# P times V in 64x32 tiles of TensorE, over two PSUM banks, with all eight banks in one pool

## The chip, the cores and the metric

The kernel runs on one core of a Trainium2 chip. Its time is the device time of one execution in microseconds (us). The kernel before takes 312.37 us (median of three runs, 312.09 to 313.11).

A core has a matrix engine, TensorE (PE in the profile, with its weight loads as PEld), three engines for elementwise work, VectorE (DVE), ScalarE (ACT) and GpSimd (POOL), and a queue that starts most transfers, SyncE (SP). TensorE adds up its results in PSUM, which has eight banks; one bank holds 512 float32 numbers in each of 128 partitions. VectorE and ScalarE read PSUM; the other working memory is SBUF.

## The reference

Two blocks read the same normalised input, and their outputs are added to the input. The sizes are S = 2048 rows, D = 640, F = 1536, 32 heads of 20 columns, and a window of 256 keys.

```python
xn = _layernorm(x, axis=-1)
return x + _A_ref(xn, A_wqkv, A_wo) + _B_ref(xn, B_w_gate, B_w_up, B_w_down)

# _A_ref: attention in a sliding window
qkv = (x @ wqkv).reshape(B, S, 3, H, Dh)            # q, k, v: 32 heads of 20
scores = jnp.einsum("bhqd,bhkd->bhqk", q, k) * (Dh ** -0.5)
mask = (idx[:, None] - idx[None, :] >= 0) & (idx[:, None] - idx[None, :] < W)   # W = 256
p = _softmax(jnp.where(mask, scores, -1e9), axis=-1)
return einsum("bhqk,bhkd->bhqd", p, v).transpose(...).reshape(B, S, D) @ wo

# _B_ref: gated feed-forward
h = _sigmoid(x @ w_gate) * (x @ w_up)
return h @ w_down
```

## The kernel before

The 2048 rows are worked in four chunks of 512 (c = 0 to 3). For each chunk there are projections to q and k (`proj_block`, L302), to v (`project_v`, L330), the gate and up products (`g_gu`, L412 and L419), the down product (`down`, L433), the product with `wo` (`add_wo`, L440), and the attention. Heads are taken in eight groups of four (g = 0 to 7).

Attention is cut into steps. `scores` (L478) computes one step: it writes scores with the keys on the partitions and the queries in columns, for four heads into four banks, one head to a bank. Queries are counted in blocks of U = 64. A piece (g, hf, r, q, n, col) stands for 64 keys (half hf of the key block r) against n query blocks from block q, put at column block col. Its four matmuls, one for each head, use tiles of TensorE of 32 rows by 64 columns: the head picks one of four row groups, hf one of two column groups. So eight tiles are in use, and two pieces of different hf can stream side by side. One ScalarE instruction (L490) then takes the exponential of all four banks, 2048 columns, into the SBUF tile pT; GpSimd (`keep`, L493) sets masked entries to zero. The chunk 0 has 16 "wide" steps, two to a group; the chunks 1 to 3 have two wide steps to a group, and one "full" step without masks for each pair of groups: 76 steps in all.

`pv` (L510) multiplies P by V for one group. A piece there takes all 128 keys of a block: its four matmuls (L519), one for each head, use tiles of 128 rows by 32 columns, four of them, side by side, and all add into one bank, `acc`. Because a piece has 128 keys in a row, both halves need the same query blocks. The oldest and newest query blocks of a wide step are wanted for one half only, so GpSimd copies them, masked, to two more column blocks of pT (the entry "late", the tile has 10 blocks of 64 where PSUM has 8), and `pv` runs pieces over these. For two groups of chunks 1 to 3 that makes 80 matmuls, for two groups of chunk 0 56. `finish_group` (L527) transposes `acc` on VectorE (L529) into SBUF; `scale_group` (L535) divides by the sum of each row (L537, L541) and transposes back into `oc` (L545), of which five tiles make up a chunk, and which `add_wo` multiplies with `wo`.

The program's order is written out by hand. The loop at L718 goes through the 76 steps; between two steps it pulls "fill" (the class Fill), pieces of the projections and of the feed-forward work, by a budget of TensorE time. Before some steps (the table `due`, L710) it runs `pv` for two groups, one step after the pair's last scores (two in chunk 0). There are 15 such places in the loop, and one at the end (L760). The scaling that follows is put in a list (`fill.behind`) and issued one or two at a time with the next pieces of fill. The output of a chunk is the fill `g_out` (L464): for each of four blocks of 128 rows it computes both halves of the down product in two banks, then adds both halves of the product with `wo`, adds x (`add_x`, L444) and stores the rows.

The PSUM banks are split between two pools. `ps_d` holds four, for everything but the scores, in turn; a pool of four, `ps_h`, serves transposes at the start, and is closed for `ps_s`, one buffer of four banks for the scores, which is closed for `ps_y` at the end.

Of the kernel before, what the change touches and what calls it, by code (L numbers as in the profile page):

```python
# [9 lines left out]
P = 128  # L10
# [34 lines left out]

SPAN = 5


def wide_step(g, r, old):  # L60

    q = 2 * r
    if old:
        return dict(scores=[(g, 0, r, q, 5, 1), (g, 1, r, q + 1, 5, 2), (g, 0, r + 2, q + 4, 2, 6),
                            (g, 1, r - 2, q, 2, 0), (g, 0, r - 2, q, 1, 0), (g, 1, r + 2, q + 5, 1, 7)],
                    late=(1, 8, 2), diag=1, oldest=(0, 2),
                    pv=[(g, r, q, 5, 1), (g, r + 2, q + 4, 2, 6), (g, r, q + 5, 1, 9),
                        (g, r - 2, q, 2, 0, 8)])

    scores = [(g, 0, r, q, 5, 0), (g, 1, r, q, 6, 0)]  # L70
    if r == 0:
        scores += [(g, 0, 2, 4, 3, 5), (g, 1, 2, 5, 2, 6)]
        last = [(g, 2, 4, 3, 5)]
    else:
        scores += [(g, 0, 3, 6, 2, 5), (g, 1, 3, 7, 1, 6), (g, 0, 2, 7, 1, 7), (g, 1, 2, 7, 1, 7)]
        last = [(g, 3, 6, 2, 5), (g, 2, 7, 1, 7)]
    return dict(scores=scores, late=(5, 9, 1), diag=0, oldest=(4, 1),
                pv=[(g, r, q, 5, 0), (g, r, q + 5, 1, 9)] + last)


def full_step(gs):

    pieces = [(g, r, q, 2, 4 * n + col) for n, g in enumerate(gs) for r, q, col in ((-1, 0, 0), (2, 6, 2))]
    return dict(scores=[(g, hf, *rest) for g, *rest in pieces for hf in range(2)], pv=pieces)
# [23 lines left out]
def kernel(  # L108
# [33 lines left out]
    ps_d = pool("ps_d", 4, space=bass.MemoryType.PSUM)  # L142
    banks = ctx.enter_context(ExitStack())
    ps_h = banks.enter_context(tc.tile_pool(name="ps_h", bufs=4, space=bass.MemoryType.PSUM))

    ctx.enter_context(tc.manual_schedule())


# [94 lines left out]
    for n in (6, 4):  # L243
        ps = ps_d.tile([P, CW], FP32, name="pwarm", tag="d")
        for k in range(n):
            nc.tensor.matmul(ps, lhsT=ones[:, 0:P], rhs=ones, start=(k == 0), stop=(k == n - 1))
# [32 lines left out]
    def transpose_rows(s, copy, lo=0, hi=DC):  # L279
        pt = ps_h.tile([P, DC, P], BF16, name="pt")  # L280
        for d in range(lo, hi):
            nc.tensor.transpose(pt[:, d, :], xns[0, s][:, d * P:(d + 1) * P], ident)  # L282
        copy(out=xnT[0][:, lo:hi, s * P:(s + 1) * P], in_=pt[:, lo:hi, :])

# [10 lines left out]
    def proj_block(w, c, m):  # L295
# [3 lines left out]
        ps = ps_d.tile([P, CW], FP32, name="pqk", tag="d")  # L299
        for d in range(DC):  # L300
            wt = wqkv[:, d, base:base + D].rearrange("p (k m) -> p m k", m=DC)
            nc.tensor.matmul(ps, lhsT=wt[:, m, :], rhs=xnT[c][:, d, :],  # L302
                             start=(d == 0), stop=(d == DC - 1))
        st = stp.tile([P, CW], BF16, name="st")
        if w == "q":
            nc.vector.tensor_copy(out=st, in_=ps)
        else:
            nc.scalar.copy(out=st, in_=ps)
# [17 lines left out]
    def project_v(c, s, hf, lo=0, hi=DC, ps=None):  # L326
        if ps is None:
            ps = ps_d.tile([P, CW], FP32, name="pv", tag="d")
        for d in range(lo, hi):
            nc.tensor.matmul(ps[:, 0:HALF], lhsT=xnT[c][:, d, s * P:(s + 1) * P],  # L330
                             rhs=wqkv[:, d, 2 * D + hf * HALF:2 * D + (hf + 1) * HALF],
                             start=(d == 0), stop=(d == DC - 1))
        return ps

    def copy_v(c, s, hf, ps, copy):
        v3 = vt[c * SBC + s][:, 0:H * VW].rearrange("p (h d) -> p h d", d=VW)
        copy(out=v3[:, hf * 16:(hf + 1) * 16, 0:DH],
             in_=ps[:, 0:HALF].rearrange("p (h d) -> p h d", d=DH))
# [69 lines left out]
    def g_gu(c, f0, f1):  # L408
        for f in range(f0, f1):
            pg = ps_d.tile([P, CW], FP32, name="pg", tag="d")  # L410
            for d in range(DC):
                nc.tensor.matmul(pg, lhsT=part(wg, d, f), rhs=xnT[c][:, d, :],  # L412
                                 start=(d == 0), stop=(d == DC - 1))
            th = tp.tile([P, CW], FP32, name="th")
            nc.scalar.activation(out=th, in_=pg, func=TANH, scale=0.5)  # L415
            yield 5 * MM
            pu = ps_d.tile([P, CW], FP32, name="pu", tag="d")
            for d in range(DC):
                nc.tensor.matmul(pu, lhsT=part(wu, d, f), rhs=xnT[c][:, d, :],  # L419
# [3 lines left out]
            nc.vector.scalar_tensor_tensor(out=h, in0=th, scalar=1.0, in1=pu, op0=ADD, op1=MULT)  # L423
# [7 lines left out]
    def down(c, s, y, cut):  # L431
        for f in range(FC):
            nc.tensor.matmul(y[:, 0:cut[1] - cut[0]], lhsT=ht[c, f][:, s * P:(s + 1) * P],  # L433
# [370 lines left out]
```

## Time and profile before

| | us |
|---|---|
| median of three runs | 312.37 (312.09 to 313.11) |
| profiled execution, span from the first to the last instruction | 310.6 |
| TensorE busy (matmuls) | 303.6 (98%) |
| ScalarE busy | 192.5 (62%) |
| VectorE busy | 159.0 (51%) |
| GpSimd busy | 155.4 (50%) |
| exponentials (L490), 76 | 142.7 busy, 1.878 each |
| masks (L493), 192 | 146.8 busy |
| transposes of `acc` (L529), 32 | 21.8 busy, 0.709 each |

The profiled execution's own time is its span, 310.6 us; the runs' median has 1.8 us more, which lies around the span. The profile gives a matmul a modelled end, so the busy share of TensorE counts some overlap twice; the pace is read from starts. In the timeline a row shows the start, the time from the first start to the last end of the rows merged in it, the engine and the line. In the chain of waits (the work that ended last, followed back) a row shows the start and the time that this work adds to the chain.

### The profile page before, as it was taken

Reading aid. Unit: us, or ns where it says so; the run is one execution under the profiler, and the core shown is the slowest. Engines: PE = TensorE matmul, PEld = TensorE weight load, DVE = VectorE, ACT = ScalarE, POOL = GpSimd, SP = SyncE. Lnnn points to the kernel's source line nnn. Section 1 sums busy time; section 2 is a strip of 40 time slices with the busy share of each in tenths; the row PEclk is TensorE's granted clock in tenths of the full one; section 3 lists DMA queues with packets and bytes.
Section 4 is the critical chain, followed back from the end, with each engine's and each line's share of the span. In section 5 each row is a group of like instructions: output and inputs, shape, how many; then the busy total and the mean of one; then the engine's idle time right before and its main releaser. Section 6 shows DMA issues by size and latency. Waiting matters only on the chain.

```text
span 310.6 us, 10139 instructions
## 1 busy us (share of the span) xinstructions
PE 303.6 (98%) x4436; PEld 175.0 (56%) x4471; DVE 159.0 (51%) x313; ACT 192.5 (62%) x179; POOL 155.4 (50%) x239
## 2 busy tenths in 40 slices
PE   7999999999999999999999999999999999999996
PEld 3654444556557655644567665644546675454775
DVE  5533655639775154289826155272733526272423
ACT  6623878697763747787673647767585547768000
POOL 3000675676782827567382637546273846656000
PEclk9999999999999999999999999999999999999999
DMA  7997999765534153440035212450000220000302
GB/s 219 367 298 253 321 182 318 258 185 170 177 65 108 44 160 100 164 151 2 2 44 87 88 59 88 154 190 2 2 3 2 66 64 23 2 2 2 88 22 65
DMA packets 40301, 35.69 MB, mean 115 GB/s; under 512 B 10400, under 2 KB 39712, under 8 KB 40224
## 3 DMA queue, kind: packets, MB, share of 16 engines
q1 hardware_dynamic: 39392, 34.27, 37.6%
q10 hardware_dynamic: 864, 0.77, 0.9%
q8 instruction: 35, 0.57, 0.8%
q14 instruction: 10, 0.08, 0.1%
HBM read 23.63 MB, written 10.26 MB: 109 GB/s over the span
## 4 chain that ended last, share of the span: by engine, by line
PE 96%; issue 1%; DMA 1%; ACT 1%; DVE 0%; SPq 0%
PE y L433 17%; PE pu L419 17%; PE pg L412 17%; PE pqk L302 14%; PE ps L485 9%; PE pv L330 7%; PE y L440 7%; PE acc L519 7%; DMA xc<-in_A_x_dram 1%; PE pt L282 0%; ACT xn L614 0%; ACT xn L619 0%; DVE xn L625 0%; SPq L171 0%; ACT rstd L620 0%
## 5 line engine op out<-in xcount | busy, mean ns | idle before, releaser
L493 POOL TENSOR_SCALAR_AFFINE_SELECT pT<-pT 128x512 bf16<-128x512 bf16 (+2 forms) x192 | 146.8, 795 | 128.3 <-ACT pT L490 128.1
L490 ACT ACTIVATE pT<-ps 128x2048 bf16<-128x2048 f32 x76 | 142.7, 1878 | 64.3 <-PE ps L485 59.4
L423 DVE SCALAR_TENSOR_TENSOR h<-th,pu 128x512 bf16<-128x512 f32 x48 | 32.7, 683 | 58.2 <-PE pu L419 43.6
L419 PE MATMUL pu<-xnT,wu 128*128 128x512 bf16 x228 | 59.2, 380 | 0.7
L412 PE MATMUL pg<-xnT,wg 128*128 128x512 bf16 x226 | 58.0, 380 | 0.9 <-issue 0.5
L433 PE MATMUL y<-wd,h 128*128 128x320 bf16 (+2 forms) x396 | 57.0, 295 | 0.0
L302 PE MATMUL pqk<-xnT,wqkv 128*128 128x512 bf16 x191 | 45.7, 381 | 0.7 <-issue 0.2
L433 PEld LDWEIGHTS <-h 128*128 128x128 bf16 x396 | 36.6, 98 | 14.4
L415 ACT ACTIVATE th<-pg 128x512 f32<-128x512 f32 x48 | 28.6, 596 | 14.4 <-PE pg L412 14.0
L412 PEld LDWEIGHTS <-wg 128*128 128x128 bf16 x240 | 22.2, 98 | 25.2 <-issue 0.2
L419 PEld LDWEIGHTS <-wu 128*128 128x128 bf16 x240 | 21.9, 98 | 25.4 <-issue 0.6
L485 PEld LDWEIGHTS <-kT 20*64 20x64 bf16 x1856 | 20.6, 103 | 24.2 <-issue 22.3
L302 PEld LDWEIGHTS <-wqkv 128*128 128x128 bf16 x200 | 22.5, 119 | 18.4 <-issue 1.0
L529 DVE STREAM_TRANSPOSE t<-acc 128x512 f32<-128x512 f32 x32 | 21.8, 709 | 21.5 <-PE acc L519 21.2
L444 DVE SCALAR_TENSOR_TENSOR rows<-y,rows 128x320 bf16<-128x320 f32 x30 | 14.5, 490 | 35.2 <-PE y L440 30.2
L485 PE MATMUL ps<-qT,kT 20*64 20x128 bf16 (+4 forms) x1856 | 32.5, 239 | 0.0
L541 DVE TENSOR_TENSOR on<-t,rec 128x320 bf16<-128x320 f32 (+4 forms) x48 | 27.1, 565 | 1.1
L440 PE MATMUL y<-wo,oc 128*128 128x320 bf16 (+2 forms) x165 | 24.2, 295 | 0.0
L330 PE MATMUL pv<-wqkv,xnT 128*128 128x320 bf16 x160 | 23.7, 299 | 0.0
L519 PE MATMUL acc<-pT,v 128*32 128x128 bf16 (+3 forms) x1184 | 22.9, 231 | 0.0
L519 PEld LDWEIGHTS <-v 128*32 128x32 bf16 x1184 | 18.5, 97 | 7.5 <-issue 2.2
L440 PEld LDWEIGHTS <-oc 128*128 128x128 bf16 x165 | 15.5, 98 | 5.9
(45 smaller groups left out, 132.2 us busy)
## 6 DMA issues: line engine op xcount, KB each, us to landing
qT<-sq SPq DMA_DIRECT2D x7, 512.0 KB, 4.3
sq<-st SPq DMA_DIRECT2D x20, 128.0 KB, 3.6
sk<-st SPq DMA_DIRECT2D x20, 128.0 KB, 4.1
out_dram<-rows SPq DMA_DIRECT2D x15, 160.0 KB, 1.8
kT<-sk SPq DMA_DIRECT2D x4, 512.0 KB, 7.4
wg<-in_B_w_gate_dram SPq DMA_DIRECT2D x4, 480.0 KB, 7.1
wu<-in_B_w_up_dram SPq DMA_DIRECT2D x4, 480.0 KB, 6.1
xc<-in_A_x_dram SPq DMA_DIRECT2D x3, 640.0 KB, 5.5
```

Source lines behind the costliest of these rows:

```text
L302: nc.tensor.matmul(ps, lhsT=wt[:, m, :], rhs=xnT[c][:, d, :], start=(d == 0), stop=(d == DC - 1))
L330: nc.tensor.matmul(ps[:, 0:HALF], lhsT=xnT[c][:, d, s * P:(s + 1) * P], rhs=wqkv[:, d, 2 * D + hf * HALF:2 * D + (hf + 1) * HALF], start=( ...
L412: nc.tensor.matmul(pg, lhsT=part(wg, d, f), rhs=xnT[c][:, d, :], start=(d == 0), stop=(d == DC - 1))
L415: nc.scalar.activation(out=th, in_=pg, func=TANH, scale=0.5)
L419: nc.tensor.matmul(pu, lhsT=part(wu, d, f), rhs=xnT[c][:, d, :], start=(d == 0), stop=(d == DC - 1))
L423: nc.vector.scalar_tensor_tensor(out=h, in0=th, scalar=1.0, in1=pu, op0=ADD, op1=MULT)
L433: nc.tensor.matmul(y[:, 0:cut[1] - cut[0]], lhsT=ht[c, f][:, s * P:(s + 1) * P], rhs=wd[:, f, cut[0]:cut[1]], start=(f == 0), stop=False)
L440: nc.tensor.matmul(y[:, 0:cut[1] - cut[0]], lhsT=oc[c, m][:, s * P:(s + 1) * P], rhs=wo[:, m, cut[0]:cut[1]], start=False, stop=(m == DC - 1))
L485: nc.tensor.matmul(ps[hf * U:(hf + 1) * U, i, col * U:(col + n) * U], lhsT=qk["k", kc, g // GH][32 * i:32 * i + DH, g % GH, key:key + U], ...
L490: nc.scalar.activation(out=pt[:, :, 0:CW], in_=ps, func=EXP, scale=SCALE)
L493: nc.gpsimd.affine_select(out=out, in_=in_, pattern=[[0, HG], [0, n], [sign, width]], compare_op=GE, fill=0.0, base=base, channel_multipli ...
L519: nc.tensor.matmul(acc[32 * i:32 * i + 32, q * U:(q + n) * U], lhsT=v[:, h * VW:h * VW + 32], rhs=cols[:, i, col:col + (n - 1) * by + 1:by ...
```

## The change

P times V is cut into halves of 64 keys, with the same pieces as the scores. `pv` uses tiles of 64 rows by 32 columns, eight of them: the half of the keys picks one of two row groups, the head one of four column groups. The two halves add into two PSUM banks. `finish_group` copies the one bank to SBUF on ScalarE, adds the other on VectorE, and transposes the sum from SBUF. The copies of column blocks by GpSimd are gone, and the masks are cut anew, some over 64 partitions. In chunks 1 to 3 a pair of groups has 128 matmuls in `pv`, in chunk 0 80.

The PSUM pools become one tile of eight banks, and a list `free` in which a released bank goes to the end. Scores take four of the first six (or first four, after `pv`) banks of the list, in one run if they can. Before `pv` the fill is run on until every bank has been given back (`fill.close`), and the four banks for `pv` are chosen among the first six. `g_out` finishes a half with `wo` before it begins the next half.

```diff
 def wide_step(g, r, old):
     q = 2 * r
     if old:
-        return dict(scores=[(g, 0, r, q, 5, 1), (g, 1, r, q + 1, 5, 2), (g, 0, r + 2, q + 4, 2, 6),
-                            (g, 1, r - 2, q, 2, 0), (g, 0, r - 2, q, 1, 0), (g, 1, r + 2, q + 5, 1, 7)],
-                    late=(1, 8, 2), diag=1, oldest=(0, 2),
-                    pv=[(g, r, q, 5, 1), (g, r + 2, q + 4, 2, 6), (g, r, q + 5, 1, 9),
-                        (g, r - 2, q, 2, 0, 8)])
+        scores = [(g, 0, r, q, 5, 1), (g, 1, r, q + 1, 5, 2), (g, 0, r + 2, q + 4, 2, 6),
+                  (g, 1, r - 2, q, 2, 0), (g, 0, r - 2, q, 1, 0), (g, 1, r + 2, q + 5, 1, 7)]
+        return dict(scores=scores, pv=scores, diag=1, cut=[], oldest=(0, 2))
...
+    ps = psp.tile([P, BANKS, CW], FP32, name="ps")
+    free = list(range(BANKS))
+
+    def new_banks(n, near):
+        got = min(itertools.combinations(sorted(free[:near]), n), key=runs)
+        for k in got:
+            free.remove(k)
+        return got
+
+    def acc_first(n, near):
+        got = min(itertools.combinations(free[:near], n),
+                  key=lambda ks: runs(sorted(set(free) - set(ks))))
+        free[:] = [*got, *(k for k in free if k not in got)]
...
-            ys = [ps_d.tile([P, CW], FP32, name=f"y{i}", tag="d") for i in range(2)]
-            for y, cut in zip(ys, HALVES):
+            for cut in HALVES:
+                y = new_bank()
                 yield from down(c, s, y, cut)
-            if s == 0:
-                yield from between
-            outp(c, s, ys, rows)
-            yield 10 * 136
+                if s == 0 and cut == HALVES[0]:
+                    yield from between
+                add_wo(c, s, y, cut)
+                add_x(y, cut, rows)
+                if cut == HALVES[1]:
+                    store(c, s, rows)
+                yield 5 * 136
...
-        if "late" in step:
-            src, to, n = step["late"]
-            keep(pt[:, :, to * U:(to + n) * U].rearrange("p h (n u) -> p h n u", u=U),
-                 spans(src, n, 1), n, U, -1 - U, -1)
-            u, n = step["oldest"]
-            keep(spans(u, n, 1), spans(u, n, 1), n, U, -1, -1)
-            keep(spans(step["diag"], 2, 2), spans(step["diag"], 2, 2), 2, P, 0, 1)
+        if "diag" in step:
+            u, (o, n) = step["diag"], step["oldest"]
+            keep(spans(u + 1, 2), U, 1)
+            keep(spans(o, n), -1, -1)
+            keep(spans(o + 1, n, U, P), -1, -1)
+            keep(spans(u, 2, 0, U), 0, 1)
+            for col in step["cut"]:
+                keep(spans(col, 1, U, P), -1 - P, -1)
         return pt

     def pv(c, g, parts):
-        acc = ps_d.tile([P, CW], FP32, name="acc", tag="d")
+        halves = [new_bank() for _ in range(2)]
...
-                    acc[32 * i:32 * i + 32, q * U:(q + n) * U],
-                    lhsT=v[:, h * VW:h * VW + 32], rhs=cols[:, i, col:col + (n - 1) * by + 1:by, :],
-                    start=(k == 0), stop=(k == len(flat) - 1), skip_group_check=True)
-        finish_group(c, g, acc)
+                    ps[32 * i:32 * i + 32, halves[hf], q * U:(q + n) * U],
+                    lhsT=v[hf * U:(hf + 1) * U, h * VW:h * VW + 32],
+                    rhs=pt[hf * U:(hf + 1) * U, i, col * U:(col + n) * U],
+                    start=(k == first[hf]), stop=(k == last[hf]), skip_group_check=True)
+        finish_group(c, g, halves)

-    def finish_group(c, g, acc):
+    def finish_group(c, g, halves):
+        t0 = lop.tile([P, CW], FP32, name="t0")
         t1 = np_.tile([P, 16, 32], FP32, name="t1")
-        nc.vector.transpose(out=t1.rearrange("p b r -> p (b r)"), in_=acc)
+        nc.scalar.copy(out=t0, in_=ps[:, halves[0], :])
+        nc.vector.tensor_tensor(out=t0, in0=ps[:, halves[1], :], in1=t0, op=ADD)
+        for k in halves:
+            give(k)
+        nc.vector.transpose(out=t1.rearrange("p b r -> p (b r)"), in_=t0)
...
+        def close(self):
+            while len(free) < BANKS:
+                self.one()
...
         if t in due:
+            fill.close()
             fill.flush()
+            acc_first(2 * len(due[t]), len(free) - 2)
...
-        made = (step, scores(c, step))
+        made = (step, scores(c, step, HG if t in due else 6))
```

## The prediction

> **What bounds the kernel now.** I read the busy shares first, then the chain of waits, then the waits, then stretches of the timeline around `pv`.
>
> Busy shares and the chain, by engine and by line:
>
> ```profile
> PE 303.6 (98%) x4436; PEld 175.0 (56%) x4471; DVE 159.0 (51%) x313; ACT 192.5 (62%) x179; POOL 155.4 (50%) x239
> ...
> PE 96%; issue 1%; DMA 1%; ACT 1%; DVE 0%; SPq 0%
> PE y L433 17%; PE pu L419 17%; PE pg L412 17%; PE pqk L302 14%; PE ps L485 9%; PE pv L330 7%; PE y L440 7%; PE acc L519 7%; DMA xc<-in_A_x_dram 1%; PE pt L282 0%; ACT xn L614 0%; ACT xn L619 0%; DVE xn L625 0%; SPq L171 0%; ACT rstd L620 0%
> ```
>
> The chain is TensorE for 96%, and no other engine is over 62% busy. So a microsecond less on TensorE is a microsecond less of time, if no wait takes its place; 7%, some 21.7 us, is `pv`.
>
> The waits of TensorE on others:
>
> ```profile
> PEld L485 <- issue: 22.3, 61, 0.4
> ...
> PEld L519 <- issue: 2.2, 7, 0.4
> ...
> PEld L519 <- ACT pT L490: 1.7, 4, 0.4
> ```
>
> All are 0.4 at longest: that is the change of tile shape, no wait for data. The timeline around a score step shows it:
>
> ```profile
> 151.19 1.24 PE L419 MATMUL pu<-xnT,wu 128*128 128x512 bf16 x5
> ...
> 152.36 0.43 PE L485 MATMUL ps<-qT,kT 20*64 20x320 bf16 x24
> 152.72 1.25 PE L412 MATMUL pg<-xnT,wg 128*128 128x512 bf16 x5
> 152.97 1.88 ACT L490 ACTIVATE pT<-ps 128x2048 bf16<-128x2048 f32 x1 [0.98 <-PE ps L485]
> ```
>
> Five matmuls of 512 columns take 1.08 (the chain's row below, 0.216 each). So they end at 152.27, and the scores start 0.09 later: the change of shape. Scores start to next start is 0.36: 0.09 for changing back and 0.27 of streaming. Each tile then streams 5 + 2 + 1 blocks of 64 = 512 columns, which at full pace take 0.216. So eight tiles do run side by side here, with 0.05 lost in a step. Scores end at 152.63; the exponential starts 0.34 later.
>
> The chain's rows for `pv` in chunk 0, and in a later chunk with a product and a score step:
>
> ```profile
> 81.72 1.11 PE acc L519 x56
> ```
> ```profile
> 151.35 1.08 PE pu L419 x5
> 152.43 0.36 PE ps L485 x24
> ...
> 164.85 1.45 PE acc L519 x80
> ```
>
> Each holds one change of shape, so streaming is 1.02 and 1.36. A pair of groups later than chunk 0 has 48 blocks in each tile = 3072 columns = 6 x 0.216 = 1.30, plus 0.06. Chunk 0 has 36 blocks = 2304 columns = 0.97, plus 0.05.
>
> **The change, part by part.** The counts of other matmuls, score steps and changes of shape (169) stay, so do the DMAs and their order on SP; 0 for these.
>
> *Streaming of `pv`.* With halves apart and both row groups busy, a later pair needs 4 wide steps of 8 blocks and 8 blocks of the full step: 40 blocks = 2560 columns = 1.08. Chunk 0 needs 32 blocks = 2048 columns = 0.86. To this comes the loss: 0.05 per pair as now, at most 0.05 for every three rounds as in a score step (16 rounds, 0.29). I take 0.08, nearest to the `pv` row, whose 20 rounds are the like of these. That gives 1.16 against 1.36 and 0.94 against 1.02: 12 x 0.20 + 4 x 0.08 = 2.7 us gained; 3.2 with 0.05, and nothing with a third of 0.05 for each round (1.37 and 1.03).
>
> [...]
>
> *The first refill of a bank.* ScalarE must now copy one half (32 copies of 128x512; the nearest row, tanh L415, is 0.596), and VectorE add the other (nearest L423, 0.683). The bank of the first half is the first that the fill takes after the scores that follow `pv`. From that half's end TensorE has the second group (0.58) and a score step with both changes (0.45) to do: 1.03, in chunk 0 0.92. Needed are 0.2 to 0.34 until ScalarE starts (tanh and scores rows), 0.6 for the copy and 0.05 to restart: 0.85 to 0.99. So it is covered by 0.04 to 0.18, and about even in chunk 0, if ScalarE is free. Its rows around the 16 calls show it free by then, save in the third, where casts of k end 0.95 after `pv` starts. I take 0.2 us for all 16; bounds 0 and 16 x 0.15 = 2.4. The second half's bank is wanted a fill piece (1.08) later, the add ends 0.7 after the copy: covered.
>
> *ScalarE's queue.* The next exponential stands behind the two copies. The second ends 0.8 after `pv` (0.2 + 0.6), where the scores, which end 0.36 after it, would let the exponential start 0.63 to 0.70 after it: 0.1 to 0.2 later against the scores. Behind it stand tanh and the next exponential, on which the next score step waits for its banks. In the stretch above it ends at 154.85 and the next scores start at 154.98, so the margin is 0.13; four `pv` calls now also take banks of the step before. I take 0.1 in all; 0 to 0.8.
>
> *VectorE and `oc` in the first output.* After `pv` VectorE has add, transpose, add, transpose, then both scalings. The cover is fill, save in the output of chunk 0, where `g_out` now wants `oc` after one half, not two. VectorE and ScalarE there, before:
>
> ```profile
> 82.06 0.69 DVE L423 SCALAR_TENSOR_TENSOR h<-th,pu 128x512 bf16<-128x512 f32 x1 [0.89 <-ACT th L415]
> 82.66 1.30 DVE L529 STREAM_TRANSPOSE t<-acc 128x512 f32<-128x512 f32 x2
> 83.89 0.21 DVE L537 RECIPROCAL rec<-t 128x16 f32<-128x16 f32 x1
> ...
> 85.34 0.24 DVE L537 RECIPROCAL rec<-t 128x16 f32<-128x16 f32 x1
> ...
> 86.37 0.71 DVE L545 STREAM_TRANSPOSE oc<-on 128x512 bf16<-128x512 bf16 x1
> ```
> ```profile
> 81.43 0.59 ACT L415 ACTIVATE th<-pg 128x512 f32<-128x512 f32 x1
> ```
>
> With `pv` at 81.65: the first copy runs 82.32 to 82.92, four VectorE instructions at 0.65 (this row's pace) from 82.98 to 85.6, the scalings take 1.45 and 1.74 as here: the last `oc` is there at 88.8 (87.08 now). TensorE reaches the fifth `wo` matmul, which reads it, after 0.94 (`pv`) + 0.45 (scores) + 12 x 0.136 (down) + 1.08 + 0.45 + 1.08 + 0.54 = 6.17, at 87.8. So it waits 1.0 us; nothing is behind it that others want soon. Bounds: 0 if one VectorE instruction less stands in front and the rest runs closer, 1.7 with one more. At the outputs of chunks 1 and 2 more than 10 us of fill lie between. At the end the last `oc` is there at 296.4, 4.0 after `pv`, and wanted 7.3 after it, behind 48 down matmuls; a copy (0.8) and two adds (1.3) more make 6.1: 0.
>
> *Masks.* GpSimd has four instructions of 512 (0.687) where a later wide step had 687 + 687 + 1103 ns: 2.75 against 2.48 us, some of them on 64 partitions. A full step and its fill lie between the last masks and `pv`, over 5 us: 0. Chunk 0's masks go from 2.1 to at most 2.9 us in steps of 2.6, with two steps before `pv`: 0 too. Without this cover it would be up to 0.8 a pair.
>
> *Order of the fill.* `fill.close` and the finer `g_out` move fill between steps; each score step keeps ten matmuls of 512, 2.16 us, ahead of it, as now: 0. Were there less, an exponential (1.88 + 0.34) would stand open.
>
> *Sum.* -2.7 + 0.2 + 0.1 + 1.0 = -1.4 us on the profiled span of 310.6: 309.2, and on the median, 1.8 above it, **311.0 us**. All cheap ends together give 309.2, all dear ends 317.3.
>
> **The rivals.**
>
> *The waits eat the gain.* Refills at 2.4, `oc` at 1.7, exponentials at 0.8 against 2.7 gained: +2.2, 314.6; half of that, 312. For it: thin margins at every `pv`. Against it: TensorE waited nowhere before, and ScalarE is idle after `pv` (1 to 3 us).
>
> *All waits but 0.3 are hidden.* 310.0. For it only that VectorE instructions overlap by some 0.07.
>
> *Instructions come too slowly (slower).* The trace shows long runs of issues only at 160 in 1.36 us, 8.5 ns each; a pair now has 256 issues in 1.16 us, 4.5 ns each. If 8.5 is the floor, a pair takes 2.18 and 1.36 us: 12 x 0.82 + 4 x 0.34 = 11.2 more, 324. It decides from 5.3 ns up. Against it: the score steps issue 48 in 0.27, 5.6 ns each, though so short a run may stand in a queue.
>
> *The halves don't stream side by side (slower).* Then a pair streams 80 and 64 blocks: 2.16 and 1.73, plus 0.08: 12 x 0.88 + 4 x 0.79 = 13.7 more, with the waits 327. Against it: scores do it with four row groups, `pv` with four column groups; no row has 64x32.
>
> **How the numbers follow.** A run of this kernel tells 0.3%, 0.94 us, from no change: faster is under 311.4, slower over 313.3. The likeliest case has 0.58 and a range of its own of 310.2 to 312.0, 0.70 of it below 311.4; the hidden wait 0.12; the eaten gain 0.13 (0.4 of it within 0.3%, 0.6 slower); slow issue 0.09; halves in turn 0.08. Faster is 0.41 + 0.12 = 0.53, slower 0.08 + 0.17 = 0.25, the same 0.22. The range of 309.5 to 315.0 goes to the eaten gain and leaves out the last two cases, 0.17; the dear ends all at once lie beyond it.
>
> **What the profile after would show.** In the chain `pv` has 1.25 (128 matmuls) and 1.03 (80), with the change of shape; 2.3 or more would be one of the slower rivals. At the first output the `wo` matmuls wait about 1 us for VectorE, some 6 us after the fourth `pv`. The first fill after each `pv` starts 0.09 after the scores, or up to 0.2 with a wait on the copy. ScalarE's busy time is 19 us more, VectorE's 22, GpSimd's up to 13. What would make it wrong: a wait of TensorE that returns with every step, or a step of `pv` that isn't paced by columns.

## The result and the profile after

The changed kernel takes 335.6 us (median of four executions, 333.3 to 338.5) against 312.3 us before (312.1 to 313.1): 1.072 times as long, with a 95% interval of 1.068 to 1.076 for the ratio. The prediction was 311.0, in a range of 309.5 to 315.0. Here and below, a time is the median of all executions, and a ratio leaves out those over 1.5% longer than the fastest of the same kernel (here the one of 338.5 us). The span of the profiled execution grew from 310.6 to 333.9 us, by 23.3.

The busy times, the granted clock in 40 slices, the instruction transfers and the chain of waits, from the page after:

```profile
PE 311.9 (93%) x5143; PEld 178.2 (53%) x5143; DVE 185.7 (56%) x345; ACT 210.5 (63%) x211; POOL 176.1 (53%) x311
...
PEclk9999999999999999969999799999999999999999
...
q8 instruction: 40, 0.66, 0.9%
...
PE 77%; DVE 10%; issue 5%; DMA 3%; ACT 2%; SPq 2%; DVEq 0%; ACTq 0%
```

TensorE was 96% of the chain before; now it is 77%. VectorE, "issue" (TensorE waited for nothing that the profile shows), a DMA and SP's queue have come into it, and the clock, full before, falls in two slices.

`pv` itself is not the loss. Its rows in the chain after, one of chunk 0 and one of a later pair (some of the 80 and 128 matmuls are left out of the count), and the row behind the second:

```profile
44.76 0.99 PE ps L549 x66
...
135.39 1.39 PE ps L549 x109
137.10 5.08 issue
```

From the first of `pv` to the first of the scores the usual time is 0.99 and 1.39, against 1.11 and 1.45 before: a gain of 4 x 0.12 + 12 x 0.06 = 1.2 us at most (three later pairs took 1.45 to 1.49). The loss is in gaps of TensorE. I listed each place where two matmuls in a row start further apart than their columns take at full clock (0.216 us for 512, plus 0.09 for a change of shape), by 0.06 us or more, from 12 us on. Such gaps, with what the lower clock costs, come to 22.4 us:

| gap of TensorE after | us |
|---|---|
| inside the score step behind `pv`, no engine as releaser: at 58, 137, 204 and 296 us | 1.0 + 5.1 + 1.1 + 1.4 = 8.6 |
| inside the score step behind `pv`, VectorE waits for x's rows: at 101 and 180 us | 1.1 + 3.5 = 4.6 |
| half the clock behind the gaps of 5.1 and 3.5 | 2.3 + 1.6 = 3.9 |
| fifth `wo` matmul waits for the last `oc` of chunk 0, at 90 us | 1.7 |
| eight of 0.1 to 0.9, for VectorE's `h`, its copies of v or its adds | 3.6 |

The rest, some 2 us if the gain of `pv` is added to the 23.3, is before 12 us or in smaller gaps, and I have not placed it.

TensorE around the largest gap, from the timeline after:

```profile
135.32 1.47 PE L549 MATMUL ps<-pT,v 64*32 64x320 bf16 x128
136.72 0.38 PE L505 MATMUL ps<-qT,kT 20*64 20x320 bf16 x12
142.19 0.37 PE L505 MATMUL ps<-qT,kT 20*64 20x128 bf16 x12 [5.08 <-issue]
142.49 2.31 PE L435 MATMUL ps<-xnT,wu 128*128 128x512 bf16 x5
```

Twelve of the step's 24 matmuls go out; the other twelve write to the same four banks and stand 5 us. Five matmuls of 512 columns then take 2.3 us instead of 1.1. The stretches around it, under the view's own heading of columns:

```profile
core 0: us, PE busy (x) PEld busy (x) DVE busy (x) ACT busy (x) POOL busy (x), PEclk, DMA share, GB/s
126.00:134.00 8.00, 8.00 (x105) 5.12 (x103) 2.83 (x5) 6.82 (x9) 6.94 (x14) 1.00 0.55 165
134.00:139.80 5.80, 3.10 (x148) 1.93 (x146) 2.85 (x5) 2.98 (x5) 1.04 (x7) 1.00 0.78 245
139.80:142.10 2.30, 0.00 (x0) 0.00 (x0) 0.00 (x0) 0.00 (x0) 0.00 (x0) 0.62 0.10 34
142.10:147.00 4.90, 4.82 (x30) 1.66 (x37) 2.09 (x5) 1.90 (x2) 2.22 (x4) 0.50 0.01 3
```

From 139.8 to 142.1 no engine has an instruction. In stretches of 1 us the clock is 1.00 up to 140, 0.69 from 140 to 141, 0.50 from 141 to 147 and 0.90 from 147 to 148; at the gap of 3.5 us it is 1.00 up to 184, 0.87 from 184 to 185, 0.50 from 185 to 188 and 0.92 from 188 to 189. So these two gaps were followed by half the clock, and those of 1.7 us and less were not (1.00 behind each). Among the experiments, a gap of 1.8 us (rows a block ahead, 289 us) and one of 2.1 (shift and rows ahead, 174 us) were followed by it too: the mean clock is 0.66 from 291 to 296 us in the first, and 0.994 over the whole execution in the second. One of 3.0 (shift by 196, 174 us) and one of 2.1 (old product with copy and add, 176 us) were not followed by it, with 1.000 over the whole execution in both, so the length of a gap alone does not decide.

The other large cause, from the waits after:

```profile
DVE rows L461 <- DMA rows<-in_A_x_dram: 24.1, 6, 6.4
...
PE ps L505 <- issue: 8.6, 4, 5.1
...
PE ps L505 <- DVE rows L461: 4.5, 3, 3.4
...
PEld L457 <- DVE oc L581: 1.9, 1, 1.9
```

Before, the first of these read 5.0 us, once, and the other three had no row. The timeline at 180 us:

```profile
177.46 1.67 SPq L300 DMA_TRANSPOSE xnT<-xn  x1
...
179.17 0.58 SPq L468 DMA_DIRECT2D rows<-in_A_x_dram  x1
179.69 1.22 ACT L561 COPY t<-ps 128x512 f32<-128x512 f32 x2 [2.00 <-PE ps L549]
...
180.23 0.33 PE L505 MATMUL ps<-qT,kT 20*64 20x320 bf16 x3
183.37 0.49 DVE L461 SCALAR_TENSOR_TENSOR rows<-ps,rows 128x320 bf16<-128x320 f32 x1 [6.34 <-DMA rows<-in_A_x_dram]
183.78 0.68 DVE L562 TENSOR_TENSOR t<-ps,t 128x512 f32<-128x512 f32 x1
183.91 0.42 PE L505 MATMUL ps<-qT,kT 20*64 20x320 bf16 x21 [3.36 <-DVE rows L461]
```

SP issues the load of x's rows behind a DMA transpose. VectorE has stood 6.3 us on it with the add of x (L461), whose bank the scores want; behind it stand the adds of `pv` (L562).

### The profile page after: what moved, and what is told of

Same layout as the page of the kernel before. It is cut to its first block, busy times and chain, and to the rows that moved or that the text cites. A ratio compares the mean times of both kernels' runs of the same rounds, so it can differ in the third digit from the quotient of the medians.

```text
span 333.9 us, 11752 instructions
## 1 busy us (share of the span) xinstructions
PE 311.9 (93%) x5143; PEld 178.2 (53%) x5143; DVE 185.7 (56%) x345; ACT 210.5 (63%) x211; POOL 176.1 (53%) x311
## 3 DMA queue, kind: packets, MB, share of 16 engines
q1 hardware_dynamic: 39392, 34.27, 35.7%
## 4 chain that ended last, share of the span: by engine, by line
PE 77%; DVE 10%; issue 5%; DMA 3%; ACT 2%; SPq 2%; DVEq 0%; ACTq 0%
PE ps L427 14%; PE ps L435 14%; PE ps L450 13%; PE ps L316 12%; PE ps L505 7%; PE ps L457 6%; PE ps L344 6%; PE ps L549 5%; DVE on L577 3%; DVE t L562 2%; DMA rows<-in_A_x_dram 2%; SPq L300 1%; DVE h L439 1%; DVE t L565 1%; DVE oc L581 1%
## 5 line engine op out<-in xcount | busy, mean ns | idle before, releaser
L520 POOL TENSOR_SCALAR_AFFINE_SELECT pT<-pT 128x512 bf16<-128x512 bf16 (+3 forms) x264 | 167.6, 648 | 134.1 <-ACT pT L513 124.7
L435 PE MATMUL ps<-xnT,wu 128*128 128x512 bf16 x240 | 60.9, 385 | 0.5 <-DVE h L439 0.5
L427 PE MATMUL ps<-xnT,wg 128*128 128x512 bf16 x240 | 60.9, 385 | 0.0
L450 PE MATMUL ps<-wd,h 128*128 128x320 bf16 (+2 forms) x396 | 59.8, 299 | 0.6 <-DVE h L439 0.6
L439 DVE SCALAR_TENSOR_TENSOR h<-th,ps 128x512 bf16<-128x512 f32 x48 | 32.2, 677 | 45.9 <-PE ps L435 33.8
L316 PE MATMUL ps<-xnT,wqkv 128*128 128x512 bf16 x200 | 46.0, 381 | 0.0
L430 ACT ACTIVATE th<-ps 128x512 f32<-128x512 f32 x48 | 28.6, 596 | 19.8 <-PE ps L427 18.4
L461 DVE SCALAR_TENSOR_TENSOR rows<-ps,rows 128x320 bf16<-128x320 f32 x30 | 14.4, 488 | 43.6 <-DMA rows<-in_A_x_dram 24.1
L562 DVE TENSOR_TENSOR t<-ps,t 128x512 f32<-128x512 f32 x32 | 21.5, 672 | 24.0 <-PE ps L549 15.8
L577 DVE TENSOR_TENSOR on<-t,rec 128x320 bf16<-128x320 f32 (+4 forms) x48 | 32.6, 678 | 1.1
L316 PEld LDWEIGHTS <-wqkv 128*128 128x128 bf16 x200 | 22.4, 119 | 18.1 <-issue 0.4
L457 PE MATMUL ps<-wo,oc 128*128 128x320 bf16 (+2 forms) x165 | 26.9, 300 | 1.5 <-DVE oc L581 1.5
L344 PE MATMUL ps<-wqkv,xnT 128*128 128x320 bf16 x160 | 23.9, 299 | 0.6 <-DVE v L351 0.6
L565 DVE STREAM_TRANSPOSE t<-t 128x512 f32<-128x512 f32 x32 | 22.8, 711 | 1.1
```

Of the source, the lines that this page charges most:

```text
L316: nc.tensor.matmul(ps[:, k, :], lhsT=wt[:, m, :], rhs=xnT[c][:, d, :], start=(d == 0), stop=(d == DC - 1))
L344: nc.tensor.matmul(ps[:, k, 0:HALF], lhsT=xnT[c][:, d, s * P:(s + 1) * P], rhs=wqkv[:, d, 2 * D + hf * HALF:2 * D + (hf + 1) * HALF], star ...
L427: nc.tensor.matmul(ps[:, kg, :], lhsT=part(wg, d, f), rhs=xnT[c][:, d, :], start=(d == 0), stop=(d == DC - 1))
L435: nc.tensor.matmul(ps[:, ku, :], lhsT=part(wu, d, f), rhs=xnT[c][:, d, :], start=(d == 0), stop=(d == DC - 1))
L450: nc.tensor.matmul(ps[:, k, 0:cut[1] - cut[0]], lhsT=ht[c, f][:, s * P:(s + 1) * P], rhs=wd[:, f, cut[0]:cut[1]], start=(f == 0), stop=False)
L457: nc.tensor.matmul(ps[:, k, 0:cut[1] - cut[0]], lhsT=oc[c, m][:, s * P:(s + 1) * P], rhs=wo[:, m, cut[0]:cut[1]], start=False, stop=(m == ...
```

## The experiments

Four theories were on trial. S: TensorE's instructions are not there in time (supply). K: the single pool, half of it held by the accumulators, makes the scores wait (banks). R: VectorE's add of x comes half a block earlier than before and meets rows that are still on their way. V: copy and add lengthen VectorE's and ScalarE's queues. The runs with the rows ahead, the old product, the split in the kernel before and the finer output alone share their runs of the kernel before (312.4 us); so do the shift by 196, both together, the fill between and the old product with copy and add (312.3), and the shift by 136 and half the columns (312.2).

### Rows loaded a block ahead

```diff
+        rows_of = {0: new_rows(c, 0)}
         for s in range(SBC):
-            rows = new_rows(c, s)
+            rows = rows_of[s]
             if s == 0:
                 yield from ahead
+            if s + 1 < SBC:
+                rows_of[s + 1] = new_rows(c, s + 1)
```

> The changed kernel, with the load of x's rows for one block of the output issued a block ahead of its use; all else as it is. Theory R (VectorE's first add of x now comes half a block earlier and finds its rows not loaded; it holds the queue behind it and with it the banks): TensorE's stalls at 101 us (1.1) and 180 us (3.5) and the half clock that follows the second (1.6) go: 335.6 - 6.2 = 329.4 us, and the waits view has no row of VectorE on this load over 2 us. Rival (TensorE waits there for something else, the rows are only late beside it): 335 to 336. The stalls inside the score steps that follow a call of pv (58, 137, 204, 295 us) should stay by both.

Measured: 330.0 us (325.7 to 331.7), 5.6 less than the changed kernel. The ratio of 1.048 (1.040 to 1.055) counts the two executions of 325.7 and 329.2 us, granted clocks 0.995 and 0.989; their mean is 8 less. The other two, 330.8 and 331.7 at 0.984, lie 4 to 5 under the changed kernel's 335.6 at 0.985. The waits have no row on the load any more; what VectorE's adds wait for is TensorE:

```profile
DVE rows L461 <- PE ps L457: 33.9, 23, 2.8
...
PE ps L508 <- issue: 7.2, 4, 3.6
...
PE ps L508 <- DVE rows L461: 1.8, 1, 1.8
```

The gaps at 101 and 180 us are gone, those at 59, 136, 197 and 289 us inside the score steps are there, with 1.0, 3.6, 0.9 and 1.8 us, and half the clock behind the second and the fourth. One gap has grown, from 0.4 us (at 267 in the changed kernel) to 1.8 at 259, the last row: the scores wait for an add of x that stands behind a scaling of 1.96 us on VectorE. R holds, for 4 to 8 us; the executions lie too far apart to say it closer.

### The old product in the new pool

```diff
-        halves = [new_bank() for _ in range(2)]
+        acc = new_bank()
...
-        nc.scalar.copy(out=t0, in_=ps[:, halves[0], :])
-        nc.vector.tensor_tensor(out=t0, in0=ps[:, halves[1], :], in1=t0, op=ADD)
-        for k in halves:
-            give(k)
-        nc.vector.transpose(out=t1.rearrange("p b r -> p (b r)"), in_=t0)
+        nc.vector.transpose(out=t1.rearrange("p b r -> p (b r)"), in_=ps[:, acc, :])
+        give(acc)
```

with the pieces and masks of before.

> The changed kernel with the product of before: one bank and 160 instead of 256 TensorE instructions for a pair of groups, the score pieces and masks of before, no copy and no add; the pool in order of release, the fill's close and the finer output stay as changed. Theory S (supply: TensorE's instructions aren't there in time after 256 of them in 1.4 us): the stalls inside the score steps after pv (8.6 us by the sum at 58, 137, 204 and 295 us, and 2.0 of half clock) go, those on the rows stay: 312.4 + 6 to 7 = 318 to 320. Theory K (banks: one pool, with the accumulators taking half of it, makes the scores wait): what is lost is lost here too, 330 or more.

Measured: 313.5 us (313.0 to 315.5, ten executions; the profiled one is the longest), ratio 1.004 (1.002 to 1.006). K falls for the pool, the order of release, the fill's close and the finer output, which together cost 1.1 us. The accumulators of a pair take two banks here, not four; whether four hold the scores is left to the shifts below. What R expected of this kernel failed in part: VectorE waits for the rows as long as in the changed kernel, but TensorE loses only one gap of 1.7 us, at 171 us.

```profile
DVE rows L464 <- DMA rows<-in_A_x_dram: 25.8, 7, 5.9
...
PE ps L508 <- DVE t L559: 1.6, 1, 1.6
```

So the late load costs its 4 to 8 us only together with the new product. The likely reason, which no run isolates, is that the accumulators of a pair then take four banks, not two, and the scores come sooner to the bank that the add of x holds.

### As many instructions in the kernel before

```diff
+        cut = []
+        for k, (pt, r, q, n, col, *by) in enumerate(flat):
+            a = n // 2 if k < 8 and n > (1 if c else 2) else 0
+            cut += [(pt, r, q, a, col, *by)] if a else []
+            cut += [(pt, r, q + a, n - a, col + a * (by[0] if by else 1), *by)]
+        flat = cut
```

> The kernel before, with pieces of the product cut in two along the queries, so that a later pair of groups has 128 matmuls (256 instructions) in place of 80 and chunk 0 has 80 in place of 56, as many as the changed kernel; the same columns are streamed into the same banks, and nothing else is touched. Theory S: stalls with no engine as their cause inside the score steps after some calls of pv, 1 to 5 us each, 7 to 13 in all with the clock: 319 to 326. Theory K: no bank or wait is changed, so 312.4, or up to 314 if the smaller pieces stream at 10 ns for each two instructions.

Measured: 317.35 us (317.3 to 317.6), ratio 1.016 (1.013 to 1.018): 5.0 us for instructions alone. `pv` takes 1.47 instead of 1.45, and there are three gaps, of 1.0, 1.8 and 1.6 us, at 132, 186 and 276 us. The first, from the timeline:

```profile
130.55 1.54 PE L525 MATMUL acc<-pT,v 128*32 128x128 bf16 x128
132.02 0.38 PE L485 MATMUL ps<-qT,kT 20*64 20x320 bf16 x12
133.39 0.28 PE L485 MATMUL ps<-qT,kT 20*64 20x128 bf16 x12 [0.98 <-issue]
```

S holds: the same stop after twelve matmuls of the same step as in the changed kernel, with no bank, copy or output changed. It is less than was expected (7 to 13): the stops are shorter, and the granted clock stays at 1.000.

### Where the stops stand

Counting TensorE's instructions in the program, every one of these stops (those that have no engine as releaser) comes after an index of 195 more than a multiple of 256 (194 in one case). The page counts 35 transfers of instructions on q8 before, and 40 after, of 16 KB each (0.66 MB / 40); TensorE has some 8,960 and 10,300 instructions (twice its weight loads, 4,471 and 5,143, and a few more), so one transfer goes with 256 of them. In the table a block is 256 instructions up to the index; "transfer" is the next one of 16 KB in the trace:

```
kernel         index  block begun  used up        transfer        goes on   gap
changed         1219     54.1       58.4 (4.3)   57.27 to 58.25    59.68    1.2
changed         4035    135.4      136.8 (1.4)  139.90 to 140.86  142.19    5.4
changed         6083    202.9      204.3 (1.5)  203.04 to 204.28  205.63    1.3
changed         7363    240.2      241.6 (1.4)  238.03 to 239.23  241.62    none
changed         9411    294.1      295.5 (1.4)  294.77 to 295.78  297.10    1.6
before, split   4035    130.7      132.1 (1.4)  130.98 to 131.92  133.39    1.3
before, split   6082    184.5      186.1 (1.6)  186.06 to 187.00  188.33    2.2
before, split   7363    222.9      224.4 (1.5)  220.49 to 221.47  224.38    none
before, split   9411    274.5      276.0 (1.4)  275.43 to 276.34  277.77    1.8
```

Where a block is used up in 1.4 to 1.6 us, and the next transfer begins only after that block was begun, TensorE stands, and goes on 1.3 to 1.5 us after the transfer's end; where the transfer came earlier it does not stand. Where it stands so, 2.7 to 3.8 us pass from the start of the block until it goes on, 6.8 in the longest case, and a block used up in 1.4 to 1.6 us doesn't cover that. (The first row is another case: its block lasted 4.3 us, and the transfer began 3.2 us into it.) `pv` of a later pair and its scores are 256 + 48 = 304 instructions in 1.75 us, so a whole block may lie inside; before they were 160 + 48 = 208, and none could. That makes a test: where the blocks lie can be moved.

### The stream shifted by 196, by 136

```diff
+        for j in range(98 if n == 4 else 0):
+            i = j % 4
+            nc.tensor.matmul(ps[32 * i:32 * i + 32, k, 0:32], lhsT=ones[0:U, 0:32], rhs=ones[0:U, 0:32],
+                             start=True, stop=True)
         give(k)
```

(behind the second warm-up; 68 in place of 98 for the shift by 136).

> The changed kernel with 98 matmuls of 32 columns (196 TensorE instructions) more behind the last warm-up matmul, where TensorE waits for x anyway; nothing after them is touched, but every later instruction stands 196 places further in TensorE's stream. Theory S, made sharper by where the stalls lie: all those inside score steps with no cause stand where the stream's index is 195 more than a multiple of 256, and at the four from 136 us on the 256 instructions before were used up in 1.4 us, or would have been: stream blocks of 256, and one that lies wholly within pv and its scores (304 instructions) is used up before the next has come. With 196 added no block lies wholly in such a stretch: the stalls at 137, 204 and 295 us (5.1 + 2.0 of half clock, 1.1, 1.4) and probably that at 58 us (1.0) go: 335.6 - 10 = 326 us, 325 to 328. Theory K (banks, semaphores or the halves themselves hold the scores): they stay where they are in the work, 335 to 336.

Measured: 327.2 us (325.0 to 328.9), ratio 1.046 (1.041 to 1.052), 8.3 less than the changed kernel. The gaps at 204 and 296 us are gone; two remain, both at an index of 195 more than a multiple of 256: 1.5 us at 139 us, in the next score step, where 218 of a block's 256 instructions lie in the `pv` and scores before, and 1.2 us at 46 us, which the rule does not explain: its block lasted 6.1 us, and TensorE goes on some 2.5 us after the transfer's end. The step that had stood 5.1 us goes through:

```profile
134.98 1.46 PE L553 MATMUL ps<-pT,v 64*32 64x320 bf16 x128
136.37 0.43 PE L509 MATMUL ps<-qT,kT 20*64 20x320 bf16 x24
```

> The changed kernel with 68 matmuls in place of 98 behind the warm-up, a shift of 136 instructions. Theory S with blocks of 256: a block now lies wholly within pv and its scores at indices 3523, 4803, 6851 and 8899, which are the calls of pv that start at 118, 160, 222 and 278 us in the changed kernel and have no stall there; their score steps (0.36 us) should get one of 1 us or more each, save where the next block was asked for early, while those at 137, 204 and 295 us have none: 328 to 333 us. Theory K: the stalls stay with the calls at 137, 204 and 295 us.

Measured: 327.9 us (327.9 and 328.0), ratio 1.050 (1.047 to 1.053). The gaps at 137, 204 and 296 us are gone, and two of the four calls named have one, of 1.1 and 1.5 us:

```profile
119.42 0.41 PE L509 MATMUL ps<-qT,kT 20*64 20x320 bf16 x19
120.92 0.23 PE L509 MATMUL ps<-qT,kT 20*64 20x64 bf16 x5 [1.09 <-issue]
```
```profile
154.14 0.38 PE L509 MATMUL ps<-qT,kT 20*64 20x320 bf16 x12
156.01 0.28 PE L509 MATMUL ps<-qT,kT 20*64 20x128 bf16 x12 [1.48 <-issue]
```
```profile
214.17 1.47 PE L553 MATMUL ps<-pT,v 64*32 64x320 bf16 x128
215.56 0.43 PE L509 MATMUL ps<-qT,kT 20*64 20x320 bf16 x24
```

The steps stop after 19 and 12 matmuls, at 3523 and 4803. The third, at 6851, and the fourth, at 8899, go through: there the transfer began at 212.7 and 270.4, before the block was begun at 214.2 and 271.9. That settles S for the gaps behind `pv`: nothing behind the warm-up was changed, four accumulator banks included, and where gaps came they stood where the count put them.

### Both: shifted, and the rows ahead

> The changed kernel with both the 98 warm-up matmuls that shift the stream and the load of x's rows a block ahead. If S and R are two separate causes, their gains add: 335.6 - 10 - 6 = 319.6 us, and what is left over the kernel before is VectorE's longer queue (the wait for the last oc of chunk 0 of 1.7 us, and five waits of 0.4 to 0.9 us on h, v and the banks): 317 to 321. If one was only cover for the other (the rows wait would return where the supply no longer stalls): 324 or more.

Measured: 326.0 us (324.4 to 329.2), ratio 1.044 (1.037 to 1.051): 1.3 less than the shift alone, where 6 were expected, and within the spread of either (325.0 to 328.9 with the shift). The gains do not add. At 174 us the wait on the rows (2.9 us with the shift alone) is gone, and a stop at the index 5571 = 195 + 21 x 256, of 2.1 us, has taken its place, with 1.7 us of half the clock behind it; with the shift alone TensorE stood on the rows there while the transfer came. At 139 us the stop is now 2.9 instead of 1.5 us.

### Fill between the two groups

```diff
-        for group in due.get(t, []):
+        for n, group in enumerate(due.get(t, [])):
+            if n:
+                held, fill.behind = fill.behind, []
+                fill.pull(1)
+                fill.close()
+                fill.behind = held
+                acc_first(2, len(free) - 2)
```

> The changed kernel with one piece of fill (five matmuls of 512 columns) between the products of the two groups of a pair, so that no more than 176 TensorE instructions of 64 columns or so stand in a row; two more changes of tile shape for each of 15 pairs, 15 x 0.19 = 2.8 us. Theory S: the stalls of supply go, -10 us, and +2.8: 328 us, 326 to 330. Theory K: stalls stay, +2.8: 338.

Measured: 330.3 us (328.8 to 332.1), ratio 1.058 (1.052 to 1.065). Of the stops at the index only one is left (0.7 us, at 202), as S expects, but the fill stands elsewhere now, and other gaps come: 2.5 us for GpSimd's masks at 86, 1.8 us at 113, 1.7 us at 167, with half the clock behind the first two (0.990 over the whole execution). For the supply it agrees; as a repair it is none, 18 us above the kernel before.

### The old product with copy and add

```diff
-        nc.vector.transpose(out=t1.rearrange("p b r -> p (b r)"), in_=ps[:, acc, :])
+        t0 = lop.tile([P, CW], FP32, name="t0")
+        nc.scalar.copy(out=t0, in_=ps[:, acc, :])
+        nc.vector.tensor_tensor(out=t0, in0=ps[:, acc, :], in1=t0, op=ADD)
         give(acc)
+        nc.vector.transpose(out=t1.rearrange("p b r -> p (b r)"), in_=t0)
```

(against the old product in the new pool)

> The changed kernel with the product of before (one bank, 160 instructions for a pair), but with the copy by ScalarE and the add by VectorE kept: the add takes the bank and its own copy, so it doubles both the product and the sum by which it is divided. Theory V (what is left when supply and rows are taken away is VectorE's and ScalarE's longer queue): against the same kernel without copy and add (313.5 us) the wait for the last oc of chunk 0 (1.7), those on h, v and banks (0.4 to 0.9 each, 3.4 in all) and perhaps a longer wait on the rows come back: 317 to 321. Rival (these waits come from the halves' second bank or from the masks): 313.5 to 314.5.

Measured: 318.0 us (317.9 to 321.3; the profiled execution is the longest), ratio 1.020 (1.014 to 1.026), 4.5 more than without copy and add. The wait for the last `oc` is back (1.6 us), and gaps of 0.5 to 2.1 on v, `h`, the banks and the rows:

```profile
PE ps L508 <- DVE t L561: 2.0, 1, 2.0
PEld L460 <- DVE oc L579: 1.8, 1, 1.8
...
PE ps L460 <- DVE oc L579: 1.4, 1, 1.4
PE ps L453 <- DVE rows L464: 1.3, 1, 1.3
...
PE ps L347 <- DVE v L354: 1.2, 1, 1.2
```

V holds, for 4.5 us by the medians; the gaps in the profile are those of an execution 3.3 us above its median.

### The finer output alone

```diff
-            ys = [ps_d.tile([P, CW], FP32, name=f"y{i}", tag="d") for i in range(2)]
-            for y, cut in zip(ys, HALVES):
+            for cut in HALVES:
+                y = ps_d.tile([P, CW], FP32, name="y", tag="d")
                 yield from down(c, s, y, cut)
...
-            outp(c, s, ys, rows)
-            yield 10 * 136
+                add_wo(c, s, y, cut)
+                add_x(y, cut, rows)
+                if cut == HALVES[1]:
+                    store(c, s, rows)
+                yield 5 * 136
```

(in the kernel before)

> The kernel before, with the finer output alone: each half of a block's columns gets its wo product, its add of x and gives its bank back before the other half is begun. Theory R: VectorE waits for the rows here too, several times 3 to 6 us, but the scores have banks of their own, so that TensorE loses only what the four banks of the fill cannot cover: 313 to 317. Rival (the finer output costs nothing, as predicted): 312.4, waits on the rows as before (5.0 us once).

Measured: 312.1 us (312.0 to 312.4, ten executions), ratio 0.999 (0.997 to 1.000). VectorE does wait for the rows, 15.2 us in five times against 5.0 once, and TensorE has no gap at all: the scores' banks are not those that the add of x holds.

```profile
DVE rows L444 <- DMA rows<-in_A_x_dram: 15.2, 5, 5.0
```

### Half the columns

```diff
             v = vt[c * SBC + r]
+            n = max(1, n // 2)
```

> The changed kernel with the shift by 196 instructions, and each matmul of the product cut to half its queries (5 blocks of 64 to 2, 6 to 3, 2 to 1, 1 stays), so half of the product is left out: as many instructions, 20 in place of 40 blocks of columns in each tile for a later pair. Theory I (from its second half on, pv is paced by how fast its instructions go out, 10 ns for a weight load and a matmul): the time from its first to the scores' first instruction stays at 1.3 to 1.4 us in later chunks and near 0.9 to 1.0 in chunk 0. Theory C (columns and a loss for each round): 20 blocks = 0.54, and 0.08 and the change of shape: 0.7 us. The whole time: 326 to 328 by I, 318 by C.

Measured: 328.4 us (327.0 and 329.8), ratio 1.052 (1.041 to 1.062), no faster than the shift alone. With half the columns a later pair takes 1.22 us to the scores, against 1.39:

```profile
135.43 1.22 PE ps L554 x124
```

Less the change of shape, that is 1.13 us for 256 instructions, 4.4 ns each, where the columns need 0.54. So `pv` of a later pair is paced mostly by the rate at which instructions go out, and the full columns add 0.17 us. That is the prediction's own sign of being wrong, a step of `pv` that isn't paced by columns. In chunk 0 it takes 0.83 in two of four calls, against 0.99.

## Why the prediction was wrong

Three terms failed. The supply of TensorE's instructions behind `pv` stood at 0 and cost 8.3 us by the shift; the load of x's rows against the earlier add stood at 0 and cost 4 to 8; refills, ScalarE's queue and `oc` stood at 1.3 together, and copy and add cost 4.5. Against that, `pv` gained 1.2 us at most, not 2.7. Part by part:

- *Streaming of `pv`, -2.7 us.* Right in sign, the term was mis-sized: 1.39 and 0.99 where 1.25 and 1.03 were expected, at most 1.2 us gained. The tiles of both halves do run side by side (the rival of halves in turn, 2.2 us a pair, did not come); the loss term of 0.08 is 0.22 for a later pair, where 256 instructions take 1.13 us with half the columns, and 0.04 in chunk 0.
- *"Instructions come too slowly".* This rival named the right resource, with the wrong mechanism and the chance of 0.09. It priced a steady floor of 8.5 ns for each instruction, deciding from 5.3 ns on; the runs show 4.4 ns with half the columns and 5.1 with all. What costs is that instructions come in blocks of 256, and that a block used up in 1.4 us can be gone before the next one is there. The kernel before, read for 208 instructions in a row, could not show it; the forecast took the evidence of score steps (48 in 0.27 us) for the whole, though their 5.6 ns lie above the 5.3 that decides, and so spoke for the rival, not against it. The shifts show 8 us, half clock included; the split alone in the kernel before 5.0.
- *"DMAs and their order on SP stay: 0", and "order of the fill and the finer `g_out`: 0".* The finer output alone is worth 0 (312.1); with the pool and the order it is 1.1. But the add of x now comes half a block earlier while its load stands where it stood on SP, behind DMA transposes, so VectorE waits 24.1 us instead of 5.0. I counted what SP issues and not when VectorE first needs it. The cost appears where the scores take the bank that this add holds: 5.6 us by the medians of the run with the rows ahead, 4 to 8 by its single executions.
- *VectorE and `oc` in the first output, +1.0.* The wait is where it was put, at the fifth `wo` matmul, 6.4 us after the start of `pv` (6.2 said), and 1.7 us long, the upper bound given. The last `oc` is there 8.0 us after that start instead of 7.15: scalings took 0.66, 0.79 and 0.66 us, beside masks.
- *First refill +0.2, ScalarE's queue +0.1; "nothing is behind it that others want soon".* Too small together, and not for the reason given: TensorE has no row of a wait on the copy itself. Copy and add alone cost 4.5 us, of which 1.6 is `oc`; the rest is other work in VectorE's queue (`h`, v, the adds) that comes later than TensorE wants its bank or its operand. I priced the banks of `pv` and not those of the fill behind them in the same queue. "The waits eat the gain" saw the kind of thing, with 2.2 us at most.
- *The clock.* The prediction had no gap of 1.8 us or more, the shortest that half the clock followed in these runs, and so no loss of clock. It costs 3.9 us of the profiled execution. It also spreads the executions of one kernel: those with the shift took 325.0, 327.2, 327.3 and 328.9 us at granted clocks of 1.000, 0.994, 0.990 and 0.989.
- *Masks, end of the kernel.* Nothing in the trace speaks against 0, save by way of VectorE (below). GpSimd's busy time grew by 20.7 us, where up to 13 was said.

The parts don't add exactly: 1.1 (pool), 4.5 (copy and add) and 8.3 (supply, from the shift) make 13.9 of 23.3. Of the other 9, the rows have 5.6 when taken alone, but 1.3 with the shift, where a stop of supply stood behind their wait. The shift also leaves stops of supply: with both, 2.9 and 2.1 us and 1.7 of half the clock, 6.7 of the 13.7 that remain over the kernel before. The rest stays open; what the new masks cost by way of VectorE no run measures.

## What to carry to other kernels

Count the instructions of a dense stretch, not only its columns: here 304 TensorE instructions in 1.75 us used up a block of 256 before the next was there, at places that depend on where the blocks fall and on when their transfers begin, so that adding instructions far ahead moves them. When one instruction is pulled forward, look at what it reads as well as at what it frees: a load that was in time for the old place made VectorE stand 6.3 us here, with the adds of `pv` behind it. And a wait that costs nothing while two users have their own banks can cost once they share a pool: of 24.1 us of such waits TensorE lost 4.5 here, and 1.6 of 25.8 with the old product.

## What was not expected of the hardware

TensorE's instructions arrive in transfers of 16 KB (256 instructions) on q8, most of which take 0.9 to 1.5 us (2.4 once); the page counts their time against the same 16 DMA engines as the data's, 0.9% on q8 and 35.7% on q1. At the longest stop, 5.4 us at 136.8, the transfer began 4.5 us after its block was begun; from 134 to 139.8 us the DMA engines were 78% busy, and it began as they fell idle. In the kernel before, split, the transfer at the same index began after 0.3 us. But there, too, data kept the engines 91% busy from 129 to 131 us, so busy engines do not always delay it. In the kernel before, the split one and the changed one, eleven transfers began more than 2 us after their block was begun, and in between the data's packets filled over 70% of the engines' time in each case. That the data held them up is likely; no run took the data away.

VectorE's scalings (L541 before, L577 after), which read two SBUF operands, often take longer while GpSimd masks: before, the 128x320 form has a mean of 0.49 us for the five that lie beside no mask, and 0.80 for the eleven that lie mostly beside one, up to 1.34; with the shift, one of 128x128 took 1.96, and the scores waited 1.8 us for the add of x behind it:

```profile
256.34 1.96 DVE L581 TENSOR_TENSOR on<-t,rec 128x128 bf16<-128x128 f32 x1
...
258.23 0.88 DVE L465 SCALAR_TENSOR_TENSOR rows<-ps,rows 128x320 bf16<-128x320 f32 x2
258.76 0.43 PE L509 MATMUL ps<-qT,kT 20*64 20x320 bf16 x24 [1.80 <-DVE rows L465]
```

VectorE's products that read PSUM (L423 before, L439 after) don't lengthen so: before, they have a mean of 0.69 us for the 17 that lie beside no mask and 0.68 for the 28 that lie mostly beside one, and after, 0.69 for 10 and 0.67 for 34. What makes the difference no run shows.
